# Zeroing the warm-up operand first, with a shorter first row of warm-up products, in a RetNet and MLP-Mixer kernel

## The chip, the core and the metric

The kernel runs on one core of one Trainium2 chip. The core's engines are named as in the profile: PE (TensorE, the matrix products, with its weight loads listed apart as PEld), DVE (VectorE), ACT (ScalarE), POOL (GpSimd) and SP (SyncE). PE takes operands from SBUF and writes into PSUM, here in eight banks. Each engine works through its own list of instructions in order; semaphores tie the lists together. Loads are issued by POOL, transposing transfers by SP, and stores of the output by ACT, and all of them are carried by the core's 16 DMA engines. The metric is device time in microseconds (us) of one execution, lower is better.

## The reference

Two stages follow one another. The first is a retention recurrence for 4 batches, 8 heads, 768 positions and a head width of 64; the second is a mixer block over 768 tokens and 512 channels, with a hidden width of 256 in the token step and 1536 in the channel step. All inputs and the output are float32.

```python
def _attn_ref(q, k, v):
    gamma = 1.0 - 2.0 ** (-5.0 - np.arange(H, dtype=np.float32))
    scale = 1.0 / np.sqrt(D)
    for t in range(S):
        state = gamma[None, :, None, None] * state + np.einsum('bhd,bhe->bhde', k[:, :, t], v[:, :, t])
        y[:, :, t] = scale * np.einsum('bhd,bhde->bhe', q[:, :, t], state)
    return y

def _moe_ref(x, w_tok1, w_tok2, w_ch1, w_ch2):
    xt = x.transpose(0, 2, 1)
    h = np.maximum(xt @ w_tok1, 0.0) @ w_tok2
    u = x + h.transpose(0, 2, 1)
    h2 = np.maximum(u @ w_ch1, 0.0) @ w_ch2
    return u + h2
```

The mixer's input `x` is the first stage's output with heads and head width merged into 512 channels.

## The kernel before, in words

**Tiling.** The recurrence is done in chunks of 128 positions, six to a sequence, and two heads at a time, so a batch has four pairs of heads. The function `front(b, p)` builds one pair of one batch: ACT or DVE scales k (lines 512 and 514), PE transposes k and q by products with an identity (lines 540 and 538), products of k and v give a state per chunk (line 563) which DVE sums up with decay (lines 573 and 575), PE makes the scores (line 608), DVE masks them (line 635), and PE multiplies masked scores by v and states by q (lines 652 and 649). ACT scales the result into X (line 665). Then come the token step's two products (lines 693 and 757, with the weights `wt`), the sum with X (line 764), a cast (line 772) and a transpose into uT (line 781 through DMA, or lines 791 and 797 through PE). `back(b)` does the channel step of one batch: line 826 into the hidden layer, ACT's relu on line 842, and the second product on lines 865 and 934 with their sums on DVE (lines 907 and 954). The front of batch 0 stands alone at the start; later fronts are interleaved with the backs of earlier batches.

**What sets the order.** No queue is ordered by a loop. Each piece of work is an `Op` with the engines that may do it and their estimated costs, and `arrange` plays the whole program through once when the kernel is built: every engine takes the first ready operation by a rank that is read from the string PRECEDENCE (two characters of base 36 for each operation's number). The instructions are then written out in the order of that plan. POOL's loads go through the same plan. They follow the list `ORDER`: POOL issues q, v and k of batch 0 pair by pair, then the token weights t1 and t2, and then batch 1 and the channel weights, with its own casts between.

**The warm-up products.** PE also multiplies a tile of zeros by itself into a spare bank that nobody reads (line 1069). They are written in the loop that emits the plan: wherever PE's next operation of the plan starts more than 400 ns (by the plan's own estimates) after its last one, before the plan's time 21,000, the loop puts some products in front of it, one for every 165 ns of 70% of the gap:

```python
    spare, pe_at = None, 300
            if o.start < F_ON and o.start - pe_at > 400:
                for _ in range(int((o.start - pe_at) * FILL / F_NS)):
                    nc.tensor.matmul(spare[:, :384], zero[:, :P], zero, start=True, stop=True)
```

The first such row stands at the head of PE's list. It has 23 products, and right behind it stand PE's first real instructions, the six transposes of k of batch 0's first pair (line 540), which need the identity `ident16` (line 404, DVE) and the scaled k (line 512 on ACT and line 514 on DVE). Four shorter rows follow, of 2, 2, 5 and 7 products. The tile of zeros is written by an operation of the plan, `zero_op` (line 384), which the plan puts last among DVE's steps of preparation: behind the decay constants (lines 394 to 410), the mask (line 413), three clears (line 418), the decay weights (lines 1038 and 1040), the second half of k (line 514) and the identity (line 404).

Of the kernel before, what the change touches and what calls it, by code (L numbers as in the profile page):

```python
# [10 lines left out]
FP = mybir.dt.float32  # L11
# [81 lines left out]
def arrange(ops, BUFS, BANKS, rank, fixed=None, noise=None):  # L93

# [15 lines left out]
    if fixed is None:  # L110
        for e in ENGINES:
            waiting[e].sort(key=lambda o: rank[o.n])
    else:
        waiting = {e: [o for o, x, *_ in fixed if x == e] for e in ENGINES}
        way_fix = {o.n: w for o, x, w, b in fixed}
        bank_fix = {o.n: b for o, x, w, b in fixed}
# [38 lines left out]
    def room(o):  # L155
        m, banks = 0, []
        for s in o.takes:
            if s.tag in BANKS:
                best = None
                for i in BANKS[s.tag] if fixed is None else [bank_fix[o.n][len(banks)]]:  # L160
                    if i in banks or i == 7 and t < F_ON:
                        continue
                    x = 0 if bank_slot[i] is None else slot_free(bank_slot[i])
                    if best is None or x < best[0]:
                        best = (x, i)
# [15 lines left out]
    while left:  # L181
        moved = False
        wake = INF
        for e in ENGINES:
# [4 lines left out]
            for o in w_:  # L189
# [12 lines left out]
                if fixed is not None:  # L202
                    way = way_fix[o.n]
                else:
                    way = None
                    for w in o.ways:
                        f = max(t, free[w[0]]) + w[2] + (800 if w[0] == "DVE" and t > 30000 else 300 if w[0] == "DVE" else 0)
                        if way is None or f < way[0] or (f == way[0] and w[0] == e):
                            way = (f, w)
                    if way[1][0] != e:  # L210
                        continue
                    way = way[1]
                k = 1.0 if noise is None or e == "PE" else noise.uniform(0.97, 1.1)
                start[o.n], eng[o.n], begun[o.n], way_of[o.n], bank_of[o.n] = t, e, True, way, banks
                free[e] = t + way[1] * k
                if o.dma:
                    rings.add(e, o, t)
                    if e == "SP":
                        free[e] = max(t + way[1], rings.made["SP"][-3])
                else:  # L220
                    end[o.n] = t + way[2] * k
# [15 lines left out]
        if rings.busy():  # L237
            while rings.busy() and rings.t < nxt:
                rings.step(landed)
                if landed:  # L240
                    for o, at in landed:
                        end[o.n] = at + (noise.uniform(0, 900) if noise else 0)
                        nxt = min(nxt, max(at, t + 1))
                    landed.clear()
# [18 lines left out]
    "xsldqatllmu0r37erv3xst5jcadieq4rs6123y25t201xhauk5mvkyp9gbl86jqki5djlf3rkxe4rsr49p88tuf7gafl4c0qmenxl4x1tra8"  # L263
    "h8t4cf0g6hueoqtckp0lbrgq5g1zhlgf5bdvsjg6pqlbacdc36w2h6vk7b9np3edhsqyad6rkda39afuuv2s4uj18gxpabws470x70cgumkn"
    "iao8c5anoko3wr7tsa586s35mx39ma6g8ycuvvlujdjox37um6xk86loqb669eqtlvsnefbi7oqrte0bhwrp9mbx1c1rho57w6q11oeu65dg"
    "tg7a72ep3vblswpv10ndrjaeszhbpd0oa0owwzbmhxhgembsfyw7ejlrhmwco568xq1ukbp4kiv2rq2guklpphv1o1pxlah5id4egd83iv0t"
    "x0byih1l8jw01d185vf6rthv1gcda9su5kj7142298ntvxqs30kox2dudt2ak7n8aq1nb98wq50z54fzd0wkrlprnn3jf82tttb64n7l6lp0"
    "33lcq3r6q7naezi6fkgp2dqovwcoc8mzoskan78hcifhulpkel5m48vivew3j2s2b7akwqc0gofnt7cwgluu74oy2pvu8o4050fetd692eo0"
    "k1se3tgypgheqmqd3smlv75zk952upc4pa84tv732zecrwevnb5sqfkur0u94vuy6d59v4e6axx7ckfx5r0di3910eaypc76kqa5jg7f37t5"
    "fgk0m58e3zi9obmoaze1q4fpkmuq24kkhav9ro0nuj60j4qh2jdk453mdd95hp82opu78ltxq6hfi28suwh4vo9ob5vtnk5cpzjvi0qzcbp2"  # L270
    "53vh5yvqtzkwd74k6pvfg04fccxt1m9brkdpmb31hnal9r417rar3nhrqei1xlqj5lnhrnp1pu92enskxvwjm29lxeubvr4btmh0awnyso1j"
    "iz7zh1l2bwqprikf9x1aafjhapwt633he0cvl3aan9c6v5spq2bt1pf93an52ctkjm4wks1k2brdmcas6oiofo4tsdvdkrs9ici87y94ln0c"
    "gwhh0r1ie3ah9ddecqnw62rg2o7wkcsciio9rz5q7pucmqn246incrb8rcxr9gmh71dnrhbnifrmcm4lp6bv19dofflk0jagl1xcjwjzhkm0"
    "vzjn4ibpcseo4owb4305urnr6vvs4s2qw9s06yesvjllnze589mi02geibilu607k33dwl38m1lt5a0f9jjqgtbj2xkl4g854xbku4iktw1w"
    "80ruti6kir9hfm0mhzjktf960kg3uiht0hs18mw1j92u6xijh7ls3gexl9gsm726w50ivbo4qijyptaj3lxndmdrjagzhi0629oav3vmc9wy"
    "44cerb7g9tfif0wwchthpbmuiutss7670uiy5n164pk27nfa1e13ealgfwry2nxb235ft9pep7r7qnt8vpxuhy2vv8oonoftuhoije210wnl"
    "v67du2g7m34hjbufvl7qqqjt8vig6q2fct2ykjo2czgu7ke9l66tn06caom41f2rcpeyozr8u54j1x4m3ptqnemfsf51wds85tx84a5h0s2k"
    "e7wi3w5w0pkvmdfvxmmnjcpl8bhjj328566ikt8kwm81g19snia4c1v0jlj6gkk8jsmy4y8qdz0vudgjfsix1b276wot2mvndbc38pbe7s9i"
    "4dbzc7g5tp8c7c1q619ubbjito7xsyeed3vc8fw8dx783kxj8ximebwxmk6egrt6i43oqclqcyrf2i5o5xb4itxd8uju6futs53enf7m9kds"
    "df99h2r1bduauom9ugnv9cmr8i7v8n08lxgifbnmxfq9qw7hd2d6sh75l0ehpi4zk4re1hjjpn8rs4nuoe775id8qlwgquolbqg93qdy8t9f"  # L280
    "15onmtggk6u1n1jf1vogb3qxhqf4bh8a87lwaiocssjp11xabo6aatg4ncjr643f3b32a2o64909r203t1w4dq42pjnsieetnqn3humgx52w"
    "un6bohke1tnppyp5wfofrxlhp8porrmmnjovtylya1hd6n1svyghsx5epwr5cnq0r9wax9pmtjer0ydl79bfew0a8zwnqgt0u3g2g8f2x6wh"
    "tb34sqcjx42lwun6pfsvmwsbwvrauzqvwefqjxxikga755us04o7fre2b1vasldwfclec2iwodps6zekgnj03uwpm8uxeif3ou5dngsg5pms"
    "00d17jt32h8dox3c9vb0h9cx3ibcl5dham7if59ye86mojgc9wsmsreggxsilzfjj5n4vg1yhcd9iqxgj8isu8h3q8clavtni79zd4a6wogm"
    "b217bgbamj5u97omgvliormp90khljfd20d5bu9q6ul7dappxota93f1s3ip4qkz"
# [4 lines left out]
def kernel(  # L290
# [36 lines left out]

    TURNED = 4
# [55 lines left out]
    zero_op = prep("DVE", 260, lambda: nc.vector.memset(zero, 0.0))  # L384

# [44 lines left out]
    h1_0 = const_p.tile([P, NJ, C], F16, name="h1_0")  # L430
# [14 lines left out]
    loads, x_done, uT_done, y_done, t2_done, h1_done = {}, {}, {}, {}, {}, {}  # L445
# [28 lines left out]
    def front(b, p):  # L474
        first, last = b == 0, b == 0 and p == NP - 1
        FA = "first" if first else "front"
        turned = first and p >= TURNED
# [209 lines left out]
        T1, H1 = Slot(FA), None if turned else Slot("h1")  # L687
# [10 lines left out]
        def h1_of(jt):  # L698
            return h1_0[:, jt, pc] if turned else H1.tile[:, jt]

        def emit(e):
            if turned:
                h1 = h1_0[:, :, pc]
            else:
                h1 = tile_of(H1, [P, NJ, P], F16)
# [3 lines left out]
            else:  # L709
                nc.vector.tensor_scalar(h1, a, 0.0, None, ALU.max)  # L710
        hr = op(either(emit, ACT=act(NJ * P), DVE=dve(NJ * P)),
                [t1], [] if turned else [H1], [T1])
        H1u = [] if turned else [H1]

        if turned:
            h1_done[p] = hr
            for hf in range(2):
                G = Slot(FA)

                def emit(hf=hf, G=G):  # L720
                    acc = tile_of(G, [P, 512], FP)
                    for i in range(HC):
                        nc.tensor.matmul(acc[:, i * P:(i + 1) * P], X16.tile[:, hf * HC + i], ident16,
                                         start=(i == 0), stop=False)
                gx = op(one("PE", (168, 168), emit), [cast_ops[hf]], [G], [X16])

                def emit(hf=hf, G=G):
                    for jt in range(NJ):
                        nc.tensor.matmul(G.tile[:, :SH], h1_of(jt), wt2[:, jt, hf * SH:(hf + 1) * SH],
                                         start=False, stop=(jt == NJ - 1))  # L730
                g = op(one("PE", (326, 490), emit), [hr, wops["t2"], gx], [], [G])

                def emit(e, hf=hf, G=G):
                    if UT.tile is None:
                        tile_of(UT, [P, NP, S], F16)
                    (nc.scalar.copy if e == "ACT" else nc.vector.tensor_copy)(
                        UT.tile[:, p, hf * SH:(hf + 1) * SH], G.tile[:, :SH])
                opens = (b, "uT") not in first_of
                e = op(either(emit, ACT=act(SH), DVE=dve(SH)),
                       [g, None if opens else first_of[b, "uT"]], [UT] if opens else [],  # L740
                       [G] if opens else [G, UT])
                if opens:
                    first_of[b, "uT"] = e
                uT_done[b, p, hf] = e
                x_done[b, p, hf] = x_ops[hf]
            return
        U16 = Slot("u16")
        casts = []
        for hf in range(2):
# [9 lines left out]
            t2 = op(one("PE", (336, 500), emit), [hr, wops["t2"]], [T2], H1u)  # L759
# [45 lines left out]
    def back(b):  # L805
# [42 lines left out]

        mixed = b == 0 and TURNED < NP

        def narrow(sh, blocks=range(HC)):
            H2, rel = H2s[sh], rels[sh]
            for i in blocks:
# [3 lines left out]
                for cols in cuts:  # L857
# [3 lines left out]
                    for f0 in range(0, NF, 2):  # L861
                        def emit(f0=f0, i=i, A=A, H2=H2, t=t, cols=cols, w_=w_):
                            acc = (tile_of(A, [P, 512], FP) if f0 == 0 else A.tile)[:, :w_]
                            for ft in range(f0, f0 + 2):
                                nc.tensor.matmul(acc, H2.tile[:, ft, i * P:(i + 1) * P], wc2[:, ft, cols],  # L865
                                                 start=(ft == 0), stop=(ft == NF - 1 and not mixed))
                            if mixed and f0 == NF - 2:
# [234 lines left out]
```

## Time and profile before

| | us |
|---|---|
| median of three runs (lowest, highest) | 206.23 (205.79, 206.27) |
| the profiled execution's own time | 205.96 |
| its span, first to last instruction | 204.1 |
| PE busy in the span | 185.9 (91%) |
| DVE, ACT, POOL busy | 144.3, 116.8, 113.8 |
| first real PE product starts at | 12.55 |

The span is what the profile shows; 1.86 us of the execution's own time lie outside it. Times inside the span are counted from its start. The page's second part cuts the span into 40 slices of 5.1 us. For PE it begins 0, 6, 9, 7: the engine is nearly idle in the first slice and near full in most of the later ones. The chain that ended last is followed backwards from the last instruction, and its shares tell through which lines the end was reached. Busy PE counts the warm-up products too.

### The profile page before, as it was taken

The page shows a single profiled execution, that of the slowest core. Times are in us where ns is not written, and L with a number is a line of the kernel's source. Part 1 is how long each engine was busy: PE and PEld are TensorE (multiplying, and loading weights), DVE is VectorE, ACT ScalarE, POOL GpSimd, SP SyncE. Part 2 cuts the span into 40 slices and gives each one's busy share as a digit, 9 for nine tenths or more (in the row PEclk, how much of TensorE's full clock was granted, in tenths as well). Part 3 has the DMA queues.
Part 4 walks back from the last instruction along what each step waited for, and adds up shares of the span by engine and source line. Part 5 has one row for each costly group of instructions (what it writes and reads, how often), then busy time and mean ns, then how long its engine had stood idle before and what let it go on. Part 6 is the DMA issues. An engine that isn't in the chain of part 4 may idle for free.

```text
span 204.1 us, 5153 instructions
## 1 busy us (share of the span) xinstructions
PE 185.9 (91%) x2023; PEld 139.1 (68%) x2023; DVE 144.3 (71%) x380; ACT 116.8 (57%) x272; POOL 113.8 (56%) x161
## 2 busy tenths in 40 slices
PE   0697889899899997899999999999999989999993
PEld 0365569566677887576777987876578976657682
DVE  7319999533899999975558999974319997005982
ACT  4046857789699855257988564347884102676000
POOL 8970869898999993576667973934223220000000
PEclk9999999999999999999999999999999999999999
DMA  8999999999999999999999999591300274000044
GB/s 113 151 156 167 120 173 194 131 128 181 183 155 125 145 138 186 88 139 257 124 153 148 143 113 221 79 269 32 77 3 2 74 109 176 31 3 0 0 157 154
DMA packets 104600, 25.50 MB, mean 125 GB/s; under 512 B 96768, under 2 KB 101632, under 8 KB 104576
## 3 DMA queue, kind: packets, MB, share of 16 engines
q0 software_dynamic: 77824, 13.18, 92.0%
q1 hardware_dynamic: 23152, 5.71, 24.1%
q10 hardware_dynamic: 3600, 6.29, 9.1%
q8 instruction: 16, 0.26, 0.6%
q14 instruction: 8, 0.07, 0.1%
HBM read 26.74 MB, written 6.29 MB: 162 GB/s over the span
## 4 chain that ended last, share of the span: by engine, by line
PE 57%; DVE 22%; POOL 9%; ACT 7%; issue 3%; DVEq 0%; POOLq 0%; ACTq 0%
PE bank L826 23%; PE bank L934 17%; DVE X L954 4%; DVE hs L907 4%; DVE U L575 3%; PE bank L1069 3%; DVE am L635 3%; PE bank L865 3%; PE bank L693 2%; ACT h L842 2%; PE bank L757 2%; POOL u L772 2%; DVE X L764 2%; PE bank L608 2%; POOL k L464 2%
## 5 line engine op out<-in xcount | busy, mean ns | idle before, releaser
L826 PE MATMUL bank<-uT,wc 128*128 128x384 f16 x384 | 70.6, 326 | 0.5 <-ACT uT L797 0.4
L842 ACT ACTIVATE h<-bank 128x384 f16<-128x384 f32 x96 | 44.5, 496 | 23.5 <-PE bank L826 13.0
L826 PEld LDWEIGHTS <-wc 128*128 128x128 f16 x384 | 35.4, 98 | 21.0 <-issue 1.1
L934 PEld LDWEIGHTS <-hs 128*128 128x128 f16 x264 | 24.9, 98 | 6.5 <-issue 2.2
L635 DVE TENSOR_TENSOR am<-bank,mask 128x384 f16<-128x384 f32 x40 | 20.8, 550 | 10.3 <-PE bank L608 10.3
L934 PE MATMUL bank<-wsum,hs 128*128 128x256 f16 x198 | 26.7, 273 | 0.7 <-DVE hs L907 0.4
L665 ACT ACTIVATE X<-bank,gy 128x192 f32<-128x192 f32 x60 | 21.7, 424 | 6.8 <-PE bank L652 6.2
L907 DVE TENSOR_TENSOR hs<-h 128x768 f16<-128x768 f16 x18 | 11.0, 622 | 19.6 <-ACT h L842 19.5
L772 POOL CAST u<-X 128x384 f16<-128x384 f32 x30 | 15.7, 539 | 14.1 <-DVE X L764 12.5
L575 DVE SCALAR_TENSOR_TENSOR U<-U,gp,bank 128x128 f32<-128x128 f32 x64 | 21.9, 342 | 1.6
L934 PEld LDWEIGHTS <-h 128*128 128x128 f16 x198 | 18.8, 98 | 4.6 <-issue 1.4
L954 DVE TENSOR_TENSOR X<-X,bank 128x256 f32<-128x256 f32 x55 | 21.1, 410 | 0.5 <-PE bank L934 0.4
L682 POOL CAST x<-X 128x384 f16<-128x384 f32 x22 | 12.2, 565 | 16.2 <-ACT X L665 16.2
L626 POOL TENSOR_SCALAR_AFFINE_SELECT am<-am 128x384 f16<-128x384 f16 x24 | 13.4, 576 | 12.2 <-ACT am L621 12.0
L764 DVE TENSOR_TENSOR X<-X,bank 128x384 f32<-128x384 f32 x32 | 17.1, 547 | 3.6 <-PE bank L757 3.5
L954 DVE TENSOR_TENSOR X<-X,us 128x256 f32<-128x256 f32 x44 | 18.5, 437 | 0.2 <-ACT us L970 0.2
L464 POOL DMA_DIRECT2D v<-in_v_dram x16 | 16.7, 1045 | 2.5 <-PE bank L652 2.3
L934 PE MATMUL bank<-wc,h 128*128 128x256 f16 x132 | 17.8, 272 | 0.0
L652 PE MATMUL bank<-v,am 128*128 128x64 f16 x192 | 15.0, 193 | 1.5 <-POOL am L626 0.9
L573 DVE COPY U<-bank 128x128 f32<-128x128 f32 x16 | 4.6, 285 | 15.9 <-PE bank L563 15.9
L464 POOL DMA_DIRECT2D k<-in_k_dram x15 | 15.6, 1043 | 0.1
L652 PEld LDWEIGHTS <-am 128*128 128x128 f16 x192 | 12.5, 98 | 4.2 <-POOL am L626 1.5
(71 smaller groups left out, 308.5 us busy)
## 6 DMA issues: line engine op xcount, KB each, us to landing
out_dram<-X ACTq DMA_DIRECT2D x23, 256.0 KB, 3.1
v<-in_v_dram POOLq DMA_DIRECT2D x16, 192.0 KB, 7.5
k<-in_k_dram POOLq DMA_DIRECT2D x15, 192.0 KB, 7.0
wc<-in_moe_w_ch_dram POOLq DMA_DIRECT2D x5, 512.0 KB, 8.6
q<-in_q_dram POOLq DMA_DIRECT2D x8, 192.0 KB, 5.5
q<-in_q_dram POOLq DMA_DIRECT2D x16, 96.0 KB, 8.1
wt<-in_moe_w_tok_dram POOLq DMA_DIRECT2D x2, 384.0 KB, 9.4
wc<-in_moe_w_ch_dram POOLq DMA_DIRECT2D x2, 256.0 KB, 7.1
```

Of the source, the lines that this page charges most:

```text
L464: (nc.sync if hard else nc.gpsimd).dma_start(out=tile_of(s, [P, 2, NC, D], FP if hard else F16), in_=src.rearrange("h (c p) d -> p (h c) d ...
L575: nc.vector.scalar_tensor_tensor(out=u[:, c], in0=u[:, c - 1], scalar=gp[:, p:p + 1], in1=st, op0=ALU.mult, op1=ALU.add)
L635: nc.vector.tensor_tensor(am, src, m, ALU.mult)
L652: nc.tensor.matmul(o[:, j * D:(j + 1) * D], AM[2 * hf + j].tile[:, i], V.tile[:, j, c], start=(c == 0), stop=(c == 0 or j == 1))
L665: nc.scalar.mul(X.tile[:, half(hf), h * D:(h + 1) * D], yv[:, :, j * D:(j + 1) * D], gy[:, h:h + 1])
L764: nc.vector.tensor_tensor(xo, xo, T2.tile[:, :HC * P].rearrange("p (i d) -> p i d", d=P), ALU.add)
L772: (nc.vector if e == "DVE" else nc.gpsimd).tensor_copy(U16.tile[:, half(hf)], X.tile[:, half(hf), pc])
L826: nc.tensor.matmul(acc[:, :SH], w[:, ct, (ft % FW) * P:(ft % FW + 1) * P], UT.tile[:, ct, sh * SH:(sh + 1) * SH], start=(ct == 0), stop=(c ...
L842: nc.scalar.activation(H2.tile[:, ft], A.tile[:, :SH], AF.Relu)
L907: (nc.vector if e == "DVE" else nc.gpsimd).tensor_tensor(HS.tile[:, j], x(), y(), f)
L934: nc.tensor.matmul(acc[:, half], l[:, j], r[:, j], start=(j == 0), stop=(j == K2 - 1 and not more))
L954: (nc.vector if e == "DVE" else nc.gpsimd).tensor_tensor(dst(), a_(), b_(), ALU.add)
```

## The change

The operation `zero_op` leaves the plan. In its place one memset is written ahead of everything that the plan emits, so that it is DVE's first instruction. In the loop, the plan's time from which the first gap is counted goes from 300 to 1100, and while that time is at most 2000 a product is counted as 240 ns in place of 165. The first row so has 13 products in place of 23; the four later rows keep their 2, 2, 5 and 7.

```diff
-    zero_op = prep("DVE", 260, lambda: nc.vector.memset(zero, 0.0))
...
     for o in ops:
         o.start, o.end = start[o.n], end[o.n]
+    nc.vector.memset(zero, 0.0)
     FILL, F_NS = 0.7, 165
-    spare, pe_at = None, 300
+    spare, pe_at = None, 1100
     for o, e, way, banks in order:
         if e == "PE":
             if o.start < F_ON and o.start - pe_at > 400:
                 if spare is None:
                     spare = ps.tile([P, 512], FP, name="bank7", bufs=1)
-                for _ in range(int((o.start - pe_at) * FILL / F_NS)):
+                for _ in range(int((o.start - pe_at) * FILL / (F_NS if pe_at > 2000 else 240))):
                     nc.tensor.matmul(spare[:, :384], zero[:, :P], zero, start=True, stop=True)
             pe_at = o.start + way[1]
         way[3]()
```

With one operation fewer, all later numbers fall by one, and PRECEDENCE is written anew: it is the old string without the operation's number and with every other number lowered by one, so the ranks keep their order. The rest of the diff takes out code that does nothing here: options of `arrange` that no call uses, and a variant of the token step for pairs from `TURNED = 4` on, of which there are none among pairs 0 to 3. On every engine the list of instructions stays as it was, but for the memset's new place on DVE, the ten products that PE no longer has, and one wait: PE's first transposes now wait for DVE's identity themselves, which the wait for the zeros implied before.

## The prediction

> **What bounds the kernel now.** I read the page's first parts, then the first 15 us in order of time, then who waited for whom in the first 45 us, and last the loads. From the page, the span, then PE and the DMA engines in 40 slices of 5.1 us:
>
> ```profile
> span 204.1 us, 5153 instructions
> ...
> PE   0697889899899997899999999999999989999993
> ...
> DMA  8999999999999999999999999591300274000044
> ```
>
> PE is near full from the third slice on; between 40 and 200 us it is busy 155.7 of 160 us. Time won ahead of that block and kept until 40 us therefore reaches the end. The first two slices stand out. In order of time (start, length, what, idle time and releaser):
>
> ```profile
> 5.99 0.76 DVE L404 TENSOR_SCALAR ident<-away 128x128 f16<-128x128 f32 x1
> 6.52 0.22 DVE L384 MEMSET zero<- 128x192 uint32 x1
> ...
> 6.80 5.91 PE L1069 MATMUL bank<-zero 128*128 128x384 f16 x23 [6.80 <-DVE zero L384]
> ...
> 10.30 0.15 PEld L1069 LDWEIGHTS <-zero 128*128 128x128 f16 x1 [0.17 <-issue]
> 10.62 0.15 PEld L1069 LDWEIGHTS <-zero 128*128 128x128 f16 x1 [0.17 <-issue]
> 10.92 1.40 PEld L1069 LDWEIGHTS <-zero 128*128 128x128 f16 x9 [0.15 <-issue]
> ...
> 12.55 0.50 PE L540 MATMUL bank<-ident,k 128*128 128x128 f16 x6
> ...
> 13.08 0.80 ACT L548 COPY kT<-bank 128x768 f16<-128x768 f16 x1 [7.95 <-PE bank L540]
> ...
> 14.52 0.29 DVE L573 COPY U<-bank 128x128 f32<-128x128 f32 x1 [7.78 <-PE bank L563]
> ```
>
> The zeros come last on DVE, at 6.74. The identity is done at 6.75 and the scaled k at 6.06, so the first transposes could run then; but 23 products of zeros stand ahead of them and hold PE until 12.5. ACT and DVE idle 7.95 and 7.78 us for what comes out behind that row. The products start every 0.32 us until 10.9 and every 0.16 us after that: PE reaches full speed 4.1 us into the row.
>
> Whether the rest can follow is a matter of loads. DMA engines by stretch (the last two columns are their share, in which full rate is 1.2 for weights and 2.4 for q, k and v, and GB/s):
>
> ```profile
> 12.50:20.00 7.50, 6.03 (x98) 4.36 (x95) 5.38 (x15) 5.36 (x10) 1.76 (x3) 1.00 2.68 160
> 20.00:22.00 2.00, 1.78 (x19) 1.29 (x18) 2.00 (x7) 2.00 (x7) 1.23 (x2) 1.00 1.20 208
> 22.00:23.20 1.20, 1.07 (x19) 0.76 (x19) 1.13 (x4) 1.16 (x3) 1.20 (x3) 1.00 0.31 44
> 23.20:24.50 1.30, 1.12 (x28) 0.88 (x26) 1.20 (x5) 0.69 (x2) 1.30 (x3) 1.00 2.13 133
> 24.50:26.00 1.50, 1.14 (x25) 0.82 (x21) 1.50 (x4) 0.98 (x3) 0.78 (x2) 1.00 0.83 70
> 26.00:38.00 12.00, 10.89 (x194) 9.35 (x192) 11.20 (x27) 8.51 (x19) 10.07 (x17) 1.00 1.70 182
> 38.00:42.00 4.00, 3.60 (x26) 2.13 (x25) 0.99 (x2) 2.13 (x5) 3.77 (x6) 1.00 1.43 90
> ```
>
> The queue is full until 22, nearly dry at 22 to 23.2 and at 24.5 to 26, full again until 38, thin until 42.
>
> **The change part by part.** *The zeros first.* DVE's first instruction starts at 0.85. The memset takes 0.22 us and successive memsets of this list start 0.10 apart when 0.06 long, so what follows it on DVE moves back 0.22 to 0.27 us; I take 0.25. DVE waits for no other engine between 0.85 and 6.75, so this reaches the identity in full, while the old memset at the end overlapped the identity and its removal gives back nothing there: the identity is done at 7.0. On that way ACT's first scaling does not move (its load lands at 4.4), and the decay weights wait for ACT as little as before, ACT itself following DVE. POOL and SP issue nothing later: the first 13 loads, up to 14.3, wait for no engine that moves.
>
> *The shorter row.* It can start at about 1.13 (0.06 after the zeros, as 6.74 to 6.80 before). Thirteen products at the slow 0.32 us take 4.16 us: the row ends at 5.3, before the identity. So it costs nothing, with 1.7 us of cover left; without that cover (zeros late again) it would hold the transposes for 4.16 us. Up to the last of them PE was slow before as well: 4.1 of 4.16 us, a margin of one product's fifth.
>
> *The transposes' own wait.* They wait for DVE's identity at 7.0. Behind them on PE stand two products of zeros and the q transposes, whose q landed at 5.9; ACT and DVE wait for all of these anyway. With 0.1 us from identity to first product the transposes start at 7.1 in place of 12.55: **5.45 us earlier**. This is a bound from above for the start; from below the bound is that PE is still slow there (first rival).
>
> *What is late next: loads of batch 0.* Issues and landings up to the token weights stay. Landing is issue plus the time to landing that the profile gives for that load alone. v of the second pair: 5.67 + 6.0 = 11.7, used at 16.87, room 5.2. q of the fourth pair: 9.68 + 7.4 = 17.1, used at 22.09, room 5.0. q of the third: 10.67 + 7.8 = 18.5, used at 23.66, room 5.2. Token weights t2: 13.48 + 10.3 = 23.8, used on line 757 at 28.60, room 4.8. Other loads up to there have 5.5 us or more. PE's wait for the second pair's v falls in a pause of 1.15 us that PE has at 18.47; t2's delay (0.4) falls in DVE's queue, which takes the sum of line 764 at 30.10, 0.67 after PE has made it at 29.43. The two q loads are on the way: what follows moves 5.2 us, not 5.45. The term is **-0.25 us kept back**, bounds 0 and 0.65 (t2 in full).
>
> *Then the loads that follow POOL.* POOL is freed by X (it idles 6.5 us for it until 20.77), so its further issues come 5.2 us earlier, into a queue that was dry: 1.2 us at 44 in place of 208 GB/s is 0.9 us of room, 1.5 us at 70 in place of some 180 is 0.9. These landings can come 1.8 us earlier. Channel weights issued at 28.54 land 8.6 later at 37.1 and are used at 40.66: room 3.5 + 1.8 = 5.3. The next k: 30.04 + 8.4 = 38.4, used by ACT at 42.05: 3.6 + 1.8 = 5.4. A v issued at 43.40 lands at 51.4 and is first used at 54.65: 3.2 + 1.8, and some 1.7 more from the thin stretch at 38 to 42. All exceed 5.2, if barely. If none of the dry time could be used, the room would be 3.2 to 3.5.
>
> *The tail.* From 40 us on nothing else changes: the lists are the same and the four later rows of zeros too. DMA runs thin again at 38 to 42 and 66 to 68 us, so what it was behind is caught up by then.
>
> Sum against the profiled execution: 205.96 - 5.45 + 0.25 = 200.76. That execution lies 0.27 below the median of the runs shown, 206.23, which would give 201.03. I say **201.0**.
>
> **The clock, by trace and page.** The row before: full speed came 4.1 us after its start, so on that offset the new row (1.13 to 5.3) just reaches it at 5.2. The Trainium skill ("TensorE: Matmul & The Clock Gate", Part 1, What's actually happening) says that PE runs at half clock until one busy window of about 3.4 us has passed, and that the window runs freely. By that, as an estimate, a 4.16 us row holds a whole window for only (4.16 - 3.41) / 3.41 = 22% of phases; in the other phases the sum by the Trainium skill is the 202.7 of the first rival. The trace's one row (a step at 4.1 us) agrees with the length, but cannot tell whether a window must be full.
>
> **Rivals.** *PE is still slow at 7.1.* The row ends, PE pauses 1.7 us, and the clock rises only after another 4.1 us of work, at 11.2. By then PE has done what takes half the time fast, so 2.05 us are lost and the gain is 3.15 to 3.4: **202.7**. For it: the margin of 0.06 us, and one row before is no proof that the step always comes after 4.1. Against it: the new row is as long as the slow part was. The free-running window of the Trainium skill ("TensorE: Matmul & The Clock Gate", Part 1) speaks for this rival.
>
> *The loads hold it.* If the landings from 37 us on do not move, the room of 3.2 to 3.5 us is all: **202.6**. For it: the DMA line shows 9 in nearly every slice. Against it: the two dry stretches, which POOL's wait caused.
>
> *The start was hidden anyway*, because the DMA engines set the pace of the whole first 135 us: **206.0**. Against it: rooms of 3 to 6 us ahead of every use.
>
> *Slower.* PE never gets a busy enough stretch in the first pairs, with rows of 2, 2, 5 and 7 products only, and stays slow: each slow us costs half. The gain of 5.2 is used up after 10.4 us, at 17.5; slow until 25 us would lose 8.95 in place of 5.2, **209.7**. Against it: PE was busy 6.0 of 7.5 us at 12.5 to 20 while fast, and slow it would be busy without a pause.
>
> **How the numbers follow.** Forecast 0.62 (own range 200.3 to 201.9, from the kept-back term's bounds and the loads that barely suffice); still slow 0.20; loads 0.10; hidden 0.03; slower 0.05. A measurement here tells about 0.3% (0.6 us). Faster 0.92, same 0.03, slower 0.05. The range 200.2 to 203.4 takes in the forecast and most of the first two rivals, some 0.8.
>
> **What would show it.** Right: zeros at 0.85, a row of 13 until about 5.3, transposes (line 523 now) at 7.1, ACT's first copy of kT near 7.6, the first channel product near 34.7 in place of 39.85, the DMA engines without the dry stretches, a span near 198.9. Wrong: weight loads of the first transposes 0.11 and not 0.06 us apart (slow PE); ACT or PE waiting for a load between 32 and 50 us; the transposes held by something other than the identity. What would make the number wrong most is a clock that rises late.

## The result, and the profile after

The changed kernel took 201.38 us (median of six runs, 200.74 to 201.55) against 206.24 us for the kernel before, measured beside it (six runs, 205.56 to 206.6). The ratio is 0.9765, with a 95% interval of 0.9744 to 0.9787: 4.9 us faster. The forecast was 201.0 within 200.2 to 203.4.

The profiled execution took 201.06 us with a span of 198.7, so the span fell by 5.4 us and the part outside it was 2.36 us in place of 1.86. In all executions here that part is either 1.75 to 2.0 or 2.2 to 2.45 us. The profile does not show what makes it, so I compare spans where a few tenths matter.

From the page of the changed kernel, the span and the slices (5.0 us each) of PE and of the DMA engines:

```profile
span 198.7 us, 5134 instructions
...
PE   7677798998999996999999999999999999999993
...
DMA  9999999999999999999999999592100284000034
```

PE's first digit is 7 where it was 0. The first 9 us in order of time:

```profile
0.90 0.22 DVE L972 MEMSET zero<- 128x192 uint32 x1 [0.90 <-PEq L998]
1.17 3.99 PE L981 MATMUL bank<-zero 128*128 128x384 f16 x13 [1.17 <-DVE zero L972]
...
4.34 0.15 PEld L981 LDWEIGHTS <-zero 128*128 128x128 f16 x1 [0.17 <-issue]
4.66 0.10 PEld L981 LDWEIGHTS <-zero 128*128 128x128 f16 x1 [0.17 <-issue]
...
5.98 0.76 DVE L389 TENSOR_SCALAR ident<-away 128x128 f16<-128x128 f32 x1
...
6.79 0.49 PE L523 MATMUL bank<-ident,k 128*128 128x128 f16 x6 [1.63 <-DVE ident L389]
6.79 0.32 PEld L523 LDWEIGHTS <-k 128*128 128x128 f16 x5 [0.52 <-issue]
...
7.33 0.80 ACT L531 COPY kT<-bank 128x768 f16<-128x768 f16 x1 [2.04 <-PE bank L523]
...
8.76 0.29 DVE L556 COPY U<-bank 128x128 f32<-128x128 f32 x1 [2.02 <-PE bank L546]
```

The row of zeros ends at 5.16 and PE then waits 1.63 us for DVE's identity, so the row stands in nobody's way. The identity ends at 6.74, exactly as before, although DVE now begins with the memset. The transposes start 5.76 us earlier than before, and ACT's and DVE's long pauses have shrunk from 7.95 and 7.78 us to 2.0 each. The weight loads shorten from 0.15 to 0.10 us at 4.66: in this execution PE is at full speed 3.49 us after the row began.

What the first batch waits for now: three lines, for the identity and for loads, from the waits of the first 45 us (engine and line, awaited; us in total, times, longest):

```profile
PE bank L523 <- DVE ident L389: 1.6, 1, 1.6
PEld L546 <- DMA v<-in_v_dram: 1.5, 2, 0.8
...
PEld L521 <- DMA q<-in_q_dram: 1.3, 1, 1.3
```

And the stretches that were named as decisive for the loads (busy us of PE, PEld, DVE, ACT, POOL, then clock, the DMA engines' share as in the prediction, GB/s):

```profile
12.50:20.00 7.50, 5.71 (x98) 4.19 (x97) 7.29 (x21) 6.62 (x16) 6.28 (x9) 1.00 2.53 163
...
22.00:23.20 1.20, 1.13 (x21) 0.98 (x20) 1.20 (x5) 0.38 (x1) 1.20 (x3) 1.00 2.19 160
...
24.50:26.00 1.50, 1.50 (x36) 1.47 (x34) 1.44 (x4) 1.47 (x5) 1.39 (x3) 1.00 2.23 180
```

The two dry stretches are gone (160 and 180 GB/s where there were 44 and 70). DVE is busy 7.29 of 7.5 us between 12.5 and 20, against 5.38 before. Loads are now used as they land: the issues and landings give q of the fourth pair landed 17.21 and used 17.26, q of the third 18.51 and 18.56, v of the fourth 20.08 and 20.12, the token weights t2 23.52 and 23.57. Matched instruction by instruction, the trace of after runs 5.76 us ahead of before at the first transposes, 4.8 to 5.2 on PE at the four loads just named, and 5.44 on all engines from 30 us on. The first channel products (line 770) start at 32.42, where they started at 37.86 before. The prediction named 39.85 for them, which is where a later group of them starts; that group is now at 34.40. What is won by 30 us is kept to the end.

A second set of runs of the same kernel (labelled after_again) gave 201.31 us (200.51 to 201.70, ratio 0.9754, interval 0.9725 to 0.9783) and a profile with a different start. Its expectation:

> The changed kernel once more, on the chip of the two runs beside it, as their measure. The same time as before, 201.1 to 201.7. Its profile also tells whether what it waits for in batch 0 stays the same from one execution to the next: if the landings of the loads vary, the span varies with them by some tenths.

In order of time:

```profile
1.17 4.34 PE L981 MATMUL bank<-zero 128*128 128x384 f16 x13 [1.17 <-DVE zero L972]
...
6.79 0.80 PE L523 MATMUL bank<-ident,k 128*128 128x128 f16 x6 [1.28 <-DVE ident L389]
...
8.16 0.85 PE L521 MATMUL bank<-ident,q 128*64 128x128 f16 x12
...
9.56 0.74 PE L546 MATMUL bank<-v,k 128*128 128x128 f16 x5
```

The row of 13 is slow to its end and the transposes take 0.80 in place of 0.49 us: PE ran at half speed until 10.33, as the forecast's first rival had it. That execution has a span of 199.8 and is 4.29 us ahead of before from 14 us on. Landings varied too, but they are not what made it longer: v of the fourth pair landed 1.06 us later than in after, and PE waited only 0.3 us for it. The eleven executions of this kernel have spans of 198.7 to 198.9 (four), 199.4 (two) and 199.7 to 199.8 (five). So one program had two starts, with spans 1.1 us apart. The other nine executions have no trace, and their spans alone do not tell how they started. Two of the long ones (199.4 and 199.7) had a mean granted clock of 0.989 and 0.991; it was 0.990 in the traced execution of the row of 23 below, which started fast and fell back to half speed later.

### The profile page after: what moved, and what is told of

The parts are those of the page before. It is cut to its first block, busy times and chain, and to the rows that moved or that the text cites. A ratio compares the mean times of both kernels' runs of the same rounds, so it can differ in the third digit from the quotient of the medians.

```text
span 198.7 us, 5134 instructions
## 1 busy us (share of the span) xinstructions
PE 183.9 (93%) x2013; PEld 137.9 (69%) x2013; DVE 144.7 (73%) x380; ACT 117.0 (59%) x272; POOL 113.9 (57%) x161
## 4 chain that ended last, share of the span: by engine, by line
PE 55%; DVE 24%; POOL 9%; ACT 7%; issue 3%; DVEq 0%; POOLq 0%
PE bank L770 24%; PE bank L860 17%; DVE X L877 5%; DVE hs L845 4%; DVE U L558 4%; DVE am L618 3%; PE bank L807 3%; PE bank L676 2%; ACT h L786 2%; PE bank L701 2%; POOL u L716 2%; DVE X L708 2%; PE bank L591 2%; POOL k L448 2%; PE bank L635 1%
## 5 line engine op out<-in xcount | busy, mean ns | idle before, releaser
L716 POOL CAST u<-X 128x384 f16<-128x384 f32 x30 | 15.8, 540 | 14.1 <-DVE X L708 12.5
L635 PEld LDWEIGHTS <-am 128*128 128x128 f16 x192 | 12.5, 98 | 3.5 <-POOL am L609 1.5
L701 PE MATMUL bank<-h,wt 128*128 128x128 f16 x192 | 14.5, 219 | 0.3 <-DMA wt<-in_moe_w_tok_dram 0.3
```

Of the source, the lines that this page charges most:

```text
L635: nc.tensor.matmul(o[:, j * D:(j + 1) * D], AM[2 * hf + j].tile[:, i], V.tile[:, j, c], start=(c == 0), stop=(c == 0 or j == 1))
L716: (nc.vector if e == "DVE" else nc.gpsimd).tensor_copy(U16.tile[:, half(hf)], X.tile[:, half(hf), pc])
```

## The experiments

Three theories were in play: that the gain is the row standing between identity and transposes, no more; that PE's clock at the start decides part of it; and that the loads hold back part of it. Ratios are to the kernel before, measured beside each.

**The zeros first, with the old row of 23.**

```diff
-                for _ in range(int((o.start - pe_at) * FILL / (F_NS if pe_at > 2000 else 240))):
+                for _ in range(23 if pe_at < 2000 else int((o.start - pe_at) * FILL / F_NS)):
```

> The zeros come first as in the changed kernel, but the first row keeps its 23 products. Theory (what cost was the place of the zeros: the row ran between the identity and the first transposes): the row starts at 1.17, is slow for 3.4 to 4.1 us (11 to 13 products at 0.32) and fast for the rest (0.16 each), so it ends at 6.6 to 6.9, beside the identity at 6.74. The transposes start at 6.8 to 6.95, the loads swallow what is late, and the time is that of the changed kernel, 201.4, with a span near 198.7. Rival (the ten products fewer are what pays): 1.6 to 3.2 us of the gain are gone, 203.0 to 204.6.

Measured: 201.62 us (200.91 to 202.23), ratio 0.977 (0.9746 to 0.9795), not to be told from the changed kernel's. In order of time:

```profile
1.17 5.41 PE L981 MATMUL bank<-zero 128*128 128x384 f16 x23 [1.17 <-DVE zero L972]
...
6.78 0.49 PE L523 MATMUL bank<-ident,k 128*128 128x128 f16 x6 [0.20 <-DVE ident L389]
```

The row ends 0.2 us before the identity. Once the zeros are early, ten products fewer pay nothing that can be measured. In the profiled execution PE also fell back to half speed for one stretch, behind one in which it was busy 1.98 of 3.41 us (the stretches, columns as above):

```profile
11.07:14.48 3.41, 1.98 (x39) 1.58 (x36) 3.34 (x10) 2.70 (x6) 3.18 (x4) 1.00 2.44 156
14.48:17.90 3.42, 3.42 (x18) 1.99 (x17) 3.25 (x10) 2.98 (x8) 2.91 (x5) 0.50 2.73 156
```

In that stretch the later row of seven products of zeros took 2.44 us (1.30 in after) and stood in front of the q transposes, whose q had landed at 17.12, until 17.96. The execution ended 4.84 us ahead, not 5.44. PE's full speed at the start does not settle the first 30 us for good.

**The shorter row alone**, the zeros late as before.

```diff
-                for _ in range(int((o.start - pe_at) * FILL / F_NS)):
+                for _ in range(13 if pe_at < 2000 else int((o.start - pe_at) * FILL / F_NS)):
```

> The kernel before with only the row cut to 13 products; the zeros stay behind the identity at 6.74. Theory: the row runs from 6.80 to 10.6 to 10.96, the transposes start at 10.8 to 11.1 in place of 12.55, and since every load has 4.8 us of room there the gain of 1.5 to 1.8 us comes through in full: 204.4 to 204.7. Rival (the length of the row does not matter, only when the zeros come): 206.2.

Measured: 204.63 us (ten runs, 203.72 to 205.96), ratio 0.9922 (0.99 to 0.9944). The expectation held by the median. The profiled execution was the slowest of the ten:

```profile
6.80 4.34 PE L1069 MATMUL bank<-zero 128*128 128x384 f16 x13 [6.80 <-DVE zero L384]
...
10.94 0.85 PE L540 MATMUL bank<-ident,k 128*128 128x128 f16 x6
```

Its transposes start 1.61 us earlier, but at half speed, and PE stays slow until 12.76 and is slow again from 19.58 to 23.0; nothing is left of the 1.61. So the row alone is worth 1.6 us of median with a wide scatter (spans of 201.9 to 204.2), and the zeros' place is what brings the rest.

**No first row.** The same line with 0 in place of 23.

> The changed kernel without the first row; the four later rows stay. It tells what the row of 13 is worth. Theory (it is there for PE's clock): the transposes start at 6.8 as before but slow, PE speeds up only after 3.4 to 4.1 us of work, at 10.2 to 10.9, some 1.7 to 2.0 us of PE's work are lost and the loads swallow 0.3 of that: 202.7 to 203.1, and the weight loads of the transposes are 0.11 us apart. Rival (the loads set the pace there, so a slow PE costs nothing): 201.4.

Measured: 201.67 us (201.63 to 201.69), ratio 0.9778 (0.9757 to 0.9799). My theory had 202.7 to 203.1 and missed. In order of time:

```profile
6.79 0.80 PE L523 MATMUL bank<-ident,k 128*128 128x128 f16 x6 [6.79 <-DVE ident L389]
```

PE is slow until 11.77, as the theory said. But the four spans are 199.8 or 199.9, as after_again's, so half speed at the start costs 1.1 us of span against the first profile's 198.7, not 2.05. It starts 5.76 ahead and is 4.24 ahead in the end.

**No products of zeros at all**, and no memset.

```diff
-    nc.vector.memset(zero, 0.0)
...
-                for _ in range(int((o.start - pe_at) * FILL / (F_NS if pe_at > 2000 else 240))):
+                for _ in range(0):
```

> The changed kernel without any row of warm-up products and without the zeros: what the rows are worth at all. Without the first row alone the time was 201.67, with PE fast from 11.8. Theory (the later rows, 16 products, keep PE busy enough to become and stay fast): without them PE is slow for much of the first 20 us, some 2 to 4 us of slow work more, of which the loads hide a part: 202.2 to 204. Rival (the loads hide all of it): 201.4 to 201.8.

Measured: 201.58 us (201.27 to 201.75), ratio 0.9772 (0.9747 to 0.9797): the rival's figure; the theory's 202.2 to 204 missed. In order of time:

```profile
6.79 0.80 PE L523 MATMUL bank<-ident,k 128*128 128x128 f16 x6 [6.79 <-DVE ident L389]
7.52 0.85 PE L521 MATMUL bank<-ident,q 128*64 128x128 f16 x12
8.30 0.71 PE L546 MATMUL bank<-v,k 128*128 128x128 f16 x5
```

PE stays slow until 20.50, and still the first product of v and k comes at 8.30, against 9.56 in after_again and 8.34 in the first profile of after. The later rows of zeros, which stand among these instructions, are themselves what a slow PE spends much of its time on: the first four of them take 0.85 and 0.82 us in after_again, 0.49 and 0.50 in after. All the warm-up products together are worth 0.2 to 0.3 us of median here, less than these intervals can tell from nothing. The whole measurable gain is that no row holds the transposes.

**A longer row, of 29.** The same line with 29.

> The changed kernel with a first row of 29, which ends at 7.6 to 7.9 and so holds the transposes 0.85 to 1.15 us past 6.79. Theory (the loads of batch 0 keep back what lies beyond a start of about 7.1): 0.32 us of this are swallowed, 0.5 to 0.85 come through: 201.9 to 202.2, span 199.2 to 199.6; no load is waited for at the fourth pair's q. Rival (the loads keep nothing back): all of 0.85 to 1.15 comes through, 202.3 to 202.5, span 199.6 to 199.9.

Measured: 202.0 us (201.64 to 202.43), ratio 0.9795 (0.9771 to 0.9819). In order of time, and one of the waits of the first 25 us:

```profile
1.17 6.48 PE L981 MATMUL bank<-zero 128*128 128x384 f16 x29 [1.17 <-DVE zero L972]
...
7.49 0.50 PE L523 MATMUL bank<-ident,k 128*128 128x128 f16 x6
```

```profile
PEld L521 <- DMA q<-in_q_dram: 1.9, 2, 1.7
```

The row now ends behind the identity and delays the transposes by 0.70 us. The span is longer by 1.1, since q of the fourth and third pairs landed at 18.40 and 19.75, 1.2 us later than in after, and were waited for. The median lies in the theory's range, but only as the middle of two pairs: 201.64 twice, with a span of 199.8, and 202.36 and 202.43, with 200.6. No span is within the theory's 199.2 to 199.6, and "no load is waited for" was wrong too. That the loads swallow 0.32 us is not shown by this run.

**The identity early.** Its step is emitted right behind DVE's first decay step, in place of last.

```diff
+        nc.vector.tensor_scalar(ident16, away, 0.0, None, ALU.is_equal)
...
-    ident_op = prep("DVE", 200, lambda: nc.vector.tensor_scalar(ident16, away, 0.0, None, ALU.is_equal), [away_op],
-                    (-20, 0, -1, 1))
+    ident_op = prep("DVE", 200, lambda: None, [away_op], (-20, 0, -1, 1))
```

> The changed kernel with the identity written by DVE right behind the decay constants (line 381) and not last of its preparation. Theory (from about 7.1 on the loads of batch 0 set the pace, so an earlier start is worth little): the transposes start at 6.1 to 6.8, bound by the second half of k, and the time stays within 0.3 of the changed kernel's 201.4; loads are waited for as there. Rival (the identity at 6.74 is the bound): all of the earlier start, up to 0.7 us, comes through: 200.7 to 201.0.

Measured: 201.17 us (200.92 to 201.68), ratio 0.9778 (0.9754 to 0.9801): no gain that can be told. In order of time:

```profile
2.24 0.41 DVE L382 TENSOR_SCALAR ident<-away 128x128 f16<-128x128 f32 x1
...
5.98 0.90 DVE L497 TENSOR_SCALAR k<-kf,gk 128x384 f16<-128x384 f32 x1
...
7.03 0.49 PE L523 MATMUL bank<-ident,k 128*128 128x128 f16 x6 [1.71 <-DVE k L497]
```

The identity is done at 2.65, but the second half of k slips from 5.66 to 5.98 and takes 0.90 in place of 0.40 us. The transposes wait for it and start 0.24 us later, where the theory had 6.1 to 6.8. So there was no earlier start here, and what one would be worth stays open. This execution, too, was at half speed for a stretch, from 8.39 to 11.81.

**DVE later still: the zeros written three times**, which moves DVE's list back by 0.65 us more.

```diff
-    nc.vector.memset(zero, 0.0)
+    for _ in range(3):
+        nc.vector.memset(zero, 0.0)
```

> The changed kernel with the zeros written three times, 0.45 us more work at the head of DVE. The changed kernel's identity was done at 6.74, as before the change, though DVE began its list 0.23 us later: theory, some of DVE's steps there (constants, mask, decay weights, identity) end just after POOL ends issuing a load (2.62, 3.65, 4.65, 5.69, 6.69) whenever they begin, so a delay is swallowed until a step misses its end and slips by a whole issue of 1.0 us: identity at 6.74 or at 7.7. Rival (DVE's list simply had slack of 0.23 us that is used up): identity at 7.2.

Measured: 201.44 us (two runs), ratio 0.9783 (0.9757 to 0.9809). In order of time:

```profile
0.90 0.87 DVE L973 MEMSET zero<- 128x192 uint32 x3 [0.90 <-PEq L999]
...
6.82 1.03 DVE L497 TENSOR_SCALAR k<-kf,gk 128x384 f16<-128x384 f32 x1
7.77 0.21 DVE L389 TENSOR_SCALAR ident<-away 128x128 f16<-128x128 f32 x1
...
8.03 0.49 PE L523 MATMUL bank<-ident,k 128*128 128x128 f16 x6 [1.86 <-DVE ident L389]
```

0.65 us more in front move the identity by 1.24 us, in a jump: 0.22 moved it by nothing. That is the theory's jump at POOL's issues (last section) and not the rival's 7.2, though it is 0.28 longer than expected (done at 7.98, said 7.7): it was the second half of k that was held, from 6.82 to 7.85, while POOL's issue ended at 7.66. The later start was at full PE speed, and its spans, 199.5 and 199.6, are 0.6 to 0.9 above the lowest spans of after (198.7 to 198.9).

**Two loads taken out** (q of the third pair and v of the fourth, both of batch 0, are zeros here).

```diff
-            if chunks:
+            if (b, p, what) in ((0, 2, "q"), (0, 3, "v")):
+                nc.gpsimd.memset(tile_of(s, [P, 2, NC, D], F16), 0.0)
+            elif chunks:
```

> The changed kernel without two loads of batch 0, q of the third pair and v of the fourth: POOL writes zeros into their tiles in their place, so what comes from these two is left out of the output, and the work of the engines stays. Theory (the loads up to the token weights hold batch 0): the token weights land 2 to 2.7 us earlier, the waits for loads from the fourth pair's q on vanish, and the kernel keeps all of the 5.76 us that the transposes came earlier: 0.3 to 0.6 below the changed kernel in the same job, 200.8 to 201.1. Rival (DVE's list, busy 7.3 of 7.5 us from 12.5 to 20, holds it by itself): within 0.2 of the changed kernel.

Measured: 201.54 us (200.61 to 201.75), ratio 0.9761 (0.973 to 0.9791). Of the first 35 us, one wait for a load is left:

```profile
ACT k L497 <- DMA kf<-in_k_dram: 1.5, 1, 1.5
```

t2 lands at 20.86 and is used 3 to 4 us later. With no load waited for beyond the first in this execution, the median gains nothing, and the theory's 200.8 to 201.1 missed. In the profiled execution PE was slow until 9.76, and the kernel ran 4.4 to 4.6 us ahead from 14 us on. The loads are therefore not what holds the median at 201.3 to 201.4. The rival fits: DVE is busy 7.25 of the 7.5 us at 12.5 to 20 here too, and would keep whatever delay it begins with. No run made DVE's list shorter there, so this is not shown. For a fast start the run says little: its shortest span, 198.7, is that of the changed kernel, but that execution has no trace, and q of the fourth pair, the first load waited for in after, was still loaded.

**The second pair's k loaded by SP** (as the first pair's is from the start, at 0.79) in place of POOL, so that POOL's list is shorter by one load; then the same with the identity early.

```diff
-            if chunks:
+            if (b, p, what) == (0, 1, "k"):
+                s.tile = const_p.tile([P, 2, NC, D], FP, name="kf1")
+                nc.sync.dma_start(out=s.tile, in_=src.rearrange("h (c p) d -> p (h c) d", p=P))
+            elif chunks:
```

> The changed kernel with the k of batch 0's second pair loaded as float32 by SP at the start, as the first pair's k is, so that POOL's queue has 12 loads to the token weights and not 13. Theory (the loads' pace of 1.36 us each keeps back 0.3 to 0.9 us): the later loads land about 1.3 us earlier, the waits for loads up to the token weights go, the transposes still start at 6.8, and the time falls by 0.3 to 0.6 to 200.8 to 201.1. Rival (loads are not what holds there, or SP's load only takes the same time from the DMA engines): no change, 201.4, or slower if the first q comes late.

> Both edits together: second pair's k by SP and the identity early. Theory (identity and loads bound the start one behind the other): with the loads out of the way an earlier start comes through, so this is faster than either alone: 200.2 to 200.8. Rival (something else bounds the start, the second half of k on DVE or PE's clock): as with SP's load alone, 200.8 to 201.1.

Measured: 201.83 us (201.75 to 201.88, ratio 0.9801, 0.9784 to 0.9818) and 202.06 us (201.25 to 202.63, ratio 0.9811, 0.9785 to 0.9836). Both theories missed; the first run's rival, that SP's load only takes the same time from the others, is what came. That k did land earlier, at 6.87 in place of 8.94, but it took its time from the others: the first q landed at 7.67 in place of 5.80 (8.33 in the second kernel), and q's transposes started 0.18 us later, held by it. (That t2 landed at 24.26 in place of 23.52 tells nothing: it landed at 23.52 in after and at 24.37 in after_again, one kernel.) Moved to another issuing engine, the load delayed the others all the same.

**A row of 17**, which at half speed would end at 6.6, still ahead of the identity. The same line with 17.

> The changed kernel with a first row of 17 products instead of 13. At half speed the row would end near 6.6 us, still ahead of the identity at 6.74, and it now lasts long enough that TensorE should be at full speed by 7.3 us whenever the change of speed falls. Theory (executions in which the whole row of 13 and the transposes behind it run at half speed are what keeps the median at 201.3): the first transposes at 6.8 with weight loads 0.06 us apart in every execution, span at or under 199.0, median 200.7 to 201.1. Rival (the loads and VectorE's own list set the pace of the first batch whatever TensorE's speed, as rows of 23, of none and no rows at all suggest): median 201.3 to 201.6, no difference from a row of 13 that can be told.

Measured: 200.84 us (five runs, 200.62 to 201.55), ratio 0.9747 (0.9725 to 0.9768). In order of time:

```profile
1.17 5.62 PE L981 MATMUL bank<-zero 128*128 128x384 f16 x17 [1.17 <-DVE zero L972]
...
6.79 0.62 PE L523 MATMUL bank<-ident,k 128*128 128x128 f16 x6
...
19.77 0.53 PE L521 MATMUL bank<-ident,q 128*64 128x128 f16 x12 [1.14 <-DMA q<-in_q_dram]
```

PE came to full speed at 7.08, within the transposes, as expected. The median is in the theory's range, and three of the five spans are 198.7 to 199.0. The other two are 199.6 and 199.7, and the profiled one of these shows another reason: q of the third pair landed at 19.72 (18.51 in after) and PE waited 1.14 us for it. So "at or under 199.0 in every execution" failed. The median is 0.5 us below the changed kernel's, but the intervals overlap, almost wholly with that of after_again; I do not call it faster.

## Why the prediction was right, step by step

**What bounds the kernel**: right. The gain is ahead of the block that begins near 30 us and reaches the end undiminished (5.44 at 30 us, 5.4 in span). The kernel without any warm-up product and that with the old row of 23 both show that it comes from nothing but the row no longer holding the transposes.

**The zeros first, 0.25 us of cost**: wrong, and harmless. "DVE waits for no other engine between 0.85 and 6.75, so this reaches the identity in full" is the step that failed: the identity ends at 6.74 in both traces. So the start is 5.76 us earlier, not 5.45. The waits view shows no wait there, yet several of DVE's steps end where POOL finishes issuing a load, whenever they begin.

**The shorter row costs nothing**: right, with 1.63 us of cover left (1.28 in after_again) in place of the 1.7 said. That the cover is real is shown by the row of 29, which has none.

**The loads of batch 0**: the named loads were the right ones, and the mechanism too. q of the fourth and third pairs and t2 are now used 0.05 us after they land. So is v of the fourth pair, which the prediction had not named. The term kept back was 0.32 us (5.76 to 5.44) where -0.25 was said. It is in no way fixed: q of the third pair landed between 18.2 and 19.8 in the traces of all these kernels, and in the row of 17, where it landed at 19.72, the lead fell from 5.64 to 4.35 us.

**The loads behind POOL**: right. The dry stretches were filled and the rooms sufficed, though barely: the k that the prediction names landed 0.65 us ahead of its use at 36.61, the k behind it 0.3 us ahead at 38.98, the channel weights 1.2 us ahead.

**The clock**: both cases came true, in different executions of one program. The margin of 0.06 us was no margin: full speed came 3.49 us after the row's start in after, and not within the row in after_again. The chance of 0.20 for a slow start was low by what the runs show: of the six traced kernels whose row of 13 starts at 1.17 (after, after_again, the identity early, two loads out, and the two with k by SP), PE was at full speed at the first transposes in three and slow in three. The forecast's sum fits the one (span 198.7, said 198.9). The first rival's mechanism is the other, but its price was wrong: "2.05 us are lost" was 5.76 - 4.29 = 1.47 by DVE's list, and 1.1 against the span of 198.7, because the loads, which hold back 0.32 when PE is fast, hold back nothing when it is slow. PE was slow for 3.5 us behind the identity (6.79 to 10.33), not 4.1. With half of that lost on PE, 1.77, some of it fell into its pauses.

So that 201.0 came so near the median of 201.38 is in part luck, for two reasons of opposite sign: the start came 0.31 us earlier than said, and seven of the eleven executions have spans 0.5 to 1.1 us above the shortest, which the likeliest case had left out. For one of the seven the trace shows a slow start as the reason; for the others a slow start, a later stretch at half speed (the row of 23) or a late landing (the row of 17) would do, and which it was stays open.

**The other rivals**: the loads as the bound at 202.6, a hidden start at 206.0 and a clock slow until 25 us at 209.7 did not come about. The last is the one that the runs tried: without any row PE was slow until 20.5 and the time was still 201.58. The price, half of every slow microsecond, took PE to be the bound of the first batch. Here 13.7 us of slow PE went with 1.5 us of lead lost (5.76 to 4.26), some 0.11 for each. That DVE sets the pace there is a reading and not tried by itself: it is the busier, 7.29 of the 7.5 us at 12.5 to 20 in after, and 6.82 against PE's 6.08 in the kernel without rows.

## What to carry to other kernels

Look for what stands in an in-order list ahead of the first real instruction, and ask when its operand is ready: 23 products for warming up held back the first transposes by 5.8 us because their zeros came last, and held back nothing once the zeros came first. Price a slow clock by the engine that sets the pace of that stage, not by the products' own length. And where a row just fits a threshold that one trace shows, expect both sides of it: take the spans of several executions, and a second profile, before a tenth of a microsecond is explained.

## What the runs showed of the hardware

**DVE's small steps end where POOL's load issues end.** DVE's decay step, its mask and its eight decay weights in before, and the first two issues of POOL that they overlap (start, length):

```profile
1.87 0.71 DVE L396 TENSOR_SCALAR lgs<-lgs,away 128x8 f32<-128x8 f32 x1
...
3.04 0.66 DVE L413 TENSOR_SCALAR mask<-away 128x128 f32<-128x128 f32 x1
...
3.84 1.90 DVE L1040 TENSOR_SCALAR gyw<-gyw,gy 128x64 f32<-128x64 f32 x8
```

```profile
1.39 1.23 POOL L464 DMA_DIRECT2D q<-in_q_dram  x1 [0.26 <-issue]
2.62 1.02 POOL L464 DMA_DIRECT2D v<-in_v_dram  x1
```

And in after, where they begin 0.23 us later:

```profile
2.10 0.48 DVE L381 TENSOR_SCALAR lgs<-lgs,away 128x8 f32<-128x8 f32 x1
...
3.27 0.43 DVE L398 TENSOR_SCALAR mask<-away 128x128 f32<-128x128 f32 x1
...
4.08 1.67 DVE L951 TENSOR_SCALAR gyw<-gyw,gy 128x64 f32<-128x64 f32 x8
```

The ends agree: 2.58 in both and 3.70 in both, against issues that end at 2.62 and 3.64. The delay is not yet gone there: the memset behind the mask begins at 3.25 and 3.48. It is gone with the decay weights, which begin 0.24 us apart and end at 5.74 and 5.75, over issues that end at 4.65 and 5.68; the identity then begins at 5.99 and 5.98. Where the step begins shortly behind an issue's start, as the identity at 7.77 in the kernel with three memsets (an issue of POOL there begins at 7.61), it takes 0.21 in place of 0.76 us. The Trainium skill ("SBUF — State Buffer", Who interferes with whom) says that VectorE in its two-port modes and GpSimd share one pair of ports, that whoever is first holds it for the whole instruction, and that the other is blocked. The rows above agree, with VectorE as the one that waits. The identity at 7.77 does not fit as simply, since it went through 0.16 us after an issue had begun. In which mode the steps ran no trace here shows.

**The clock's rise fits stretches of 3.41 us that do not start with the row.** Half speed, where PE fell back to it, lasted 3.41 us each time: 14.48 to 17.90 with the row of 23, 8.39 to 11.81 with the identity early, 19.58 to 23.00 with the shorter row alone. It began 10.24, 3.41 and 6.83 us behind the rise there (4.24, 4.98 and 12.76), which is three, one and two such stretches. Counted in such stretches back from the rise, in after_again PE was busy 2.34 of the 3.41 us up to 3.51 and 2.13 of the next, and stayed slow; busy 3.41 of 3.41 up to 10.33, it became fast there. In after the stretch up to 4.66 was full. The clock's record puts the rise 3.07 (the row of 23), 3.28 (the row of 29), 3.49 (after), 4.10 (before) and 5.96 us (the shorter row alone) after the row's start, and 9.16 us in after_again. The first two are shorter than a stretch, so the row need not fill one. The Trainium skill ("TensorE: Matmul & The Clock Gate", Part 1, What's actually happening) has a window of about 3.4 us that does not start with the kernel; these rows agree with that. How busy a window must be they leave open: PE's clock rose behind 2.79 of 3.41 us busy (2.72 to 6.13) with k by SP and did not behind 3.00 (6.84 to 10.26) in the kernel without rows; 1.98 of 3.41 us busy was followed by half speed in the kernel with 23 products, and 1.78 of 3.41 at 4.66 to 8.07 in after was not. The profile's clock column reads 1.00 in the slow stretches at the start, too; there the length of the weight loads (0.15 or 0.10 us) tells.

**Landings scatter.** Issued at the same time to 0.01 us, v of the fourth pair landed at 20.08, 20.39 and 21.14, and t2 at 23.52, 24.03 and 24.37, in after, the row of 17 and after_again. What sets this was not tried, and it stays open, as does the half microsecond outside the span.
